# Chunk 2's output product 3 as seven small products, and a new order of copies, differences and GpSimd work around it

## The chip, the cores and the metric

The kernel runs on one core of one Trainium2 chip. The metric is the device time of one execution in microseconds (us). A profile shows one execution: busy times and waits of the engines TensorE (PE, with its weight loads as PEld), VectorE (DVE), ScalarE (ACT), GpSimd (POOL) and of SyncE (SP), which issues most of the transfers.

## What is computed

The reference is an attention without a score matrix, followed by two dense layers with an exact GELU between them:

```python
q_s = softmax(q, axis=-1)            # q, k, v: (8 batches, 8 heads, 576, 64)
k_s = softmax(k, axis=2)             # over the sequence
kv = einsum('bhsd,bhse->bhde', k_s, v)
x = einsum('bhsd,bhde->bhse', q_s, kv)   # then (4608 tokens, 512)
h = x @ w_in                         # w_in: 512 x 2048
g = 0.5 * h * (1 + erf(h / sqrt(2)))
out = g @ w_out                      # w_out: 2048 x 512, float32
```

## The kernel before

The 4608 tokens are cut into nine chunks of 512. Chunk c below 8 holds the first 512 tokens of batch c; chunk 8 holds the last 64 tokens of all eight batches. The program order of every engine is written out by hand: each engine takes its instructions in the order in which the functions below emit them, and waits by semaphores where an operand isn't ready.

For a batch b, `exp_q` and `exp_k` (ScalarE) take the exponentials; `cast_v` turns v into bf16, in four pieces; `kv_mm` multiplies exp(k) and v in two halves of 36 small matmuls (pieces 0 and 1, then 2 and 3), and `kv_norm` (VectorE, L241) or `kv_scale` (ScalarE, L269) divides by k's sums. The sums of exp(q) are made by `reduce_sum` and a reciprocal on VectorE (`q_sums`, or `q_part` twice and `q_rest`). The scaling of exp(q) by them is done on GpSimd (`q_scale`, or `q_scale_parts`, eight instructions of 128x256). `xbar_step` transposes the scaled q with one transfer on SP's queue. `x_all` multiplies kv and the transposed q into four PSUM banks (`x_mm`) and copies these to `xT`, each by ScalarE ("s") or VectorE ("v") as its string says; `x_sums` makes differences of quarters of `xT` on VectorE.

The first dense layer of a chunk is `h_phase`, `h_pairs` or, from chunk 2 on, `h_waves` (L501). There each 2x2 block product is made by seven products instead of eight, `mm(1)` to `mm(7)`, with sums and differences of the quarters of x (`x_sums`) and of the weights (`quad_weights`). `p5_copy`, `e_sum` and `r_sum` combine the products on the way, `gelu` (ScalarE) writes `g`, and `s_parts` (VectorE) makes the differences of `g` that the second layer needs.

The second layer is again seven products, here of 16 matmuls with 256 columns each: in `y_phase` for chunks 1 and 2 (L818), `y_inner` for chunks 3 to 5, `y_inner4` for 6 and 7, `y_last` for 8. The results c11, c12, c21 and c22 are gathered in the tile `yb4` and stored in two halves by `y_store`. `y_inner` makes two of the seven products, 2 and 3, by seven smaller products once more (class `Two`, L734: seven sets of four matmuls with 128 columns). Its weight differences (`two_begin`, `two_begin4`; four GpSimd instructions each) are made once, its activation differences (`sums`, four instructions) once a chunk, for product 3 on GpSimd.

Between chunks stands `next_x` (L1350): x of the next chunk, then kv of the batch after it, while the last products of the present chunk still run. `after(i)` in `y_phase` runs the work that the caller has hung behind product i; L1336 and L1382 are the two callers. GpSimd's work of chunk 2's output is listed at L1384 and L1385: a touch that waits for VectorE's last difference (`touch_s`), `cast_v_all(4)`, `late[3]` (the last weight difference for product 2), `q_scale_parts(4)`. `four_w` holds weight differences for chunks 6 and 7, of which `h_waves` of chunks 3 to 6 make one each, at their start (L562 to L565). In `h_waves` GpSimd is released by the small copy at L622, behind `x_sums(c, (4,))`.

In chunk 0 the last of the second layer (`y_part(15, ...)`, L1291) overlaps with x of chunk 1.

Of the kernel before, what the change touches and what calls it, by code (L numbers as in the profile page):

```python
# [16 lines left out]
def kernel(  # L17
# [11 lines left out]
    nc = tc.nc  # L29
# [173 lines left out]
    def cast_v_all(b):  # L203
        for hp in range(HP):
            cast_v(b, hp, nc.gpsimd)
# [295 lines left out]
    def h_waves(c, mid, first=None):  # L501
# [19 lines left out]
        def mm(m, *qs):  # L521
            for q in qs:
                kind = {5: "B", 3: "B", 2: "C"}.get(m, "A")
                if m in (1, 5):
                    take(kind, q)
                for u in range(2):
                    for k in range(2):
                        if m in plain_w:
                            k0, t0 = plain_w[m]
                            t = 2 * q + t0 + u  # L530
                            w = wi_bf[:, k0 + k, t * 128:(t + 1) * 128]
                        else:
                            t = 2 * (q % 2) + u
                            w = quad["s"][q // 2][:, sum_w[m], k, t * 128:(t + 1) * 128]
                        nc.tensor.matmul(  # L535
                            held[kind, q][:, u], w, mov[m][:, k],
                            start=(m in (1, 5) and u == 0 and k == 0), stop=(k == 1),
                            skip_group_check=True,
                        )
# [19 lines left out]
                nc.scalar.activation(out=g[:, t:t + 2, half], in_=held[kind, q], func=AF.Gelu)  # L559

        vcopy, scopy = nc.vector.tensor_copy, nc.scalar.copy
        if 2 < c < 7:  # L562
            if c == 3:
                four_w.extend(two_begin4())
            four_w[c - 3]()  # L565
        mm(1, 0, 1)
        if first:
# [2 lines left out]
        if mid:  # L570
            seed(1)
            mm(1, 2, 3)
            mm(2, 0, 1)
            gelu("C", 0, 1)
            mm(5, 0, 1)
            p5_copy(0, scopy)
            p5_copy(1, scopy)
            x_sums(c, (3, 4))
            seed(2, vcopy)
            seed(3, vcopy)  # L580
            mm(6, 0, 1)
            e_sum(0)
            e_sum(1)
            mid()
            mm(2, 2, 3)
            gelu("C", 2, 3)
            mm(7, 0, 1)
            r_sum(0)
            r_sum(1)
            mm(3, 0, 1)  # L590
            gelu("B", 0, 1)
            mm(6, 2)
            mm(5, 2, 3)
            p5_copy(2, scopy)
            p5_copy(3, scopy)
            mm(6, 3)
            e_sum(2)
            e_sum(3)
            gelu("r", 0, 1)
            mm(4, 0, 1)  # L600
            gelu("A", 0, 1)
            mm(7, 2, 3)
            r_sum(2)
            r_sum(3)
            s_parts(c, 0, 4, (1,))
            gelu("r", 2, 3)
            mm(3, 2, 3)
            mm(4, 2, 3)
        else:
            mm(5, 0, 1)  # L610
            seed(1)
            p5_copy(0, scopy)
            p5_copy(1, scopy)
            mm(6, 0, 1)
            x_sums(c, (3,))
            if c + 2 <= B:
                q_part(c + 2, 0)
            e_sum(0)
            e_sum(1)
            x_sums(c, (4,))  # L620
            if c + 2 < B:
                nc.gpsimd.tensor_copy(out=scr[:, 2:3], in_=t4[:, 0, 0:1])  # L622
                cast_v_all(c + 2)
            mm(2, 0, 1)
            gelu("C", 0, 1)
            mm(7, 0, 1)
            r_sum(0)
            r_sum(1)
            if c + 2 <= B:
                q_part(c + 2, 1)  # L630
            mm(3, 0, 1)
            for q in (2, 3):
                mm(5, q)
                mm(1, q)
            mm(4, 0, 1)
            gelu("r", 0)
            gelu("B", 0, 1)
            gelu("r", 1)
            seed(2)
            seed(3)  # L640
            gelu("A", 0, 1)
            p5_copy(2, vcopy)
            p5_copy(3, vcopy)
            s_parts(c, 0, 4, (1,))
            mm(6, 2, 3)
            e_sum(2)
            e_sum(3)
            s_parts(c, 0, 4, (2,))
            mm(2, 2, 3)
            gelu("C", 2, 3)  # L650
            mm(7, 2, 3)
            r_sum(2)
            r_sum(3)
            gelu("r", 2, 3)
            mm(3, 2, 3)
            mm(4, 2, 3)
# [151 lines left out]
    def two_begin4():  # L808
        w = w3[:, 4:8].rearrange("p x y n -> p x (y n)")
        s = f32in.tile([128, 4, 512], BF16, tag="zs", name="two", bufs=1)  # L810
        two[4] = Two(4, *(t.rearrange("p x (i n) -> p x i n", i=4) for t in (w, s)))
        return list(two[4].weights())
# [5 lines left out]
    def y_phase(c, ins):  # L818

        act, wgt = y_operands(c)  # L820
        at = {"ya": 2, "yb": 0, "yc": 3} if c == 1 else {"ya": roles["ba"], "yb": roles["bb"], "yc": roles["x0"]}
        pa, pb, pc = (bank(at[n], n) for n in ("ya", "yb", "yc"))
        ysb = [yb4[:, 2 * i:2 * i + 2] for i in range(2)]
        c11, c12 = ysb[0][:, :, 0:HN], ysb[0][:, :, HN:DM]
        c21, c22 = ysb[1][:, :, 0:HN], ysb[1][:, :, HN:DM]

        def halves(ps):
            return ps.rearrange("p (j n) -> p j n", j=2)

        def mm(m, ps, first):  # L830
            for j in range(2):
                for k in range(HK):
                    nc.tensor.matmul(  # L833
                        ps[:, j * HN:(j + 1) * HN], act[m][:, k, j * 128:(j + 1) * 128],
                        wgt[m][:, k, :], start=(first and k == 0 and j == 0),
                        stop=(k == HK - 1), skip_group_check=True,
                    )

        def after(i):
            for fn in ins.get(i, []):  # L840
                fn()

        mm(1, pa, True)
        (nc.vector.tensor_copy if c == 1 else nc.scalar.copy)(out=c11, in_=halves(pa))
        after(1)
        mm(5, pb, True)
        nc.vector.tensor_copy(out=c22, in_=halves(pb))
        after(5)
        mm(6, pa, False)
        tt(halves(pb), halves(pa), c22)  # L850
        after(6)
        mm(2, pc, True)
        tt(c11, c11, halves(pc))
        after(2)
        mm(7, pa, False)
        tt(c22, halves(pa), c22)
        after(7)
        mm(3, pb, False)
        nc.scalar.copy(out=c12, in_=halves(pb))
        y_store(c, 0, ysb[0])  # L860
        after(3)
        mm(4, pa, False)
        nc.scalar.copy(out=c21, in_=halves(pa))
        y_store(c, 1, ysb[1])
        after(4)

    def y_inner(c, nb):

# [403 lines left out]
    def y_part(t, js):  # L1272
        for j in js:
            y_mm(0, yps[j], j, t)
# [13 lines left out]
    cast_v(1, 3, nc.scalar)  # L1288
    kv_norm(1, 0)
    y_part(14, range(J))  # L1290
    y_part(15, (0, 1, 2))  # L1291
    y_out(0, yps[0], 0)
    y_out(0, yps[1], 1, "s")
    x_tile(1, 0, Banks(5), "a")
    x_tile(1, 1, Banks(1), "h")
    x_mm(1, 0)
    kv_mm(1, 1)
    x_evac(1, 0, "s")
    x_evac(1, 1)
    kv_norm(1, 1)  # L1300
    y_part(15, (3,))

# [19 lines left out]
    for m in (3, 2, 4, 1):  # L1322
# [10 lines left out]
    exp_q(2, parts=2)  # L1333
    exp_k(2)

    y_phase(1, {  # L1336
        1: [sums[3], lambda: norm_q(2, 0, 2)],
        6: [lambda: norm_q(2, 1, 2, nc.vector), lambda: cast_v_all(3), lambda: [f() for f in two_begin(3, "vf1")], lambda: xbar_step(2), lambda: exp_q(3)],
        2: [lambda: kv_step(2), lambda: exp_k(3)],
        7: [lambda: q_sums(3)],  # L1340
        3: [lambda: table(AF.Gelu)],
        4: [lambda: load(4), lambda: load_main(5, "q", q), lambda: x_all(2, (3, 4, 1, 5)),
            lambda: kv_step(3, lambda: x_sums(2, (1,))), lambda: x_sums(2, (2,))],
    })

    def touch_s():

        nc.gpsimd.tensor_copy(out=scr[:, 2:3], in_=s12[:, HK - 1, HT:HT + 1])

    def next_x(c, nb, fn=None):  # L1350
        x_all(c + 1, [roles[n] for n in ("x0", "x1", "x2", "x3")], "svss" if fn else "svsv")
        if nb <= B:
            xbar_step(nb)
        if nb < B:
            kv_tiles(nb, (roles["kv0"], roles["kv1"]))
            if fn:
                kv_mm(nb, 0)
                kv_mm(nb, 1)
                x_sums(c + 1, (1,))
                kv_scale(nb)  # L1360
            else:
                kv_step(nb, lambda: x_sums(c + 1, (1,)))
        else:
            x_sums(c + 1, (1,))
        x_sums(c + 1, (2,))
        if fn:
            fn()

    late = []

    def q_late():
# [7 lines left out]
            fn()  # L1379

    h_waves(2, q_late)
    y_phase(2, {  # L1382
        1: [lambda: exp_q(4)],
        5: [lambda: exp_k(4), touch_s, lambda: cast_v_all(4), late[3]],  # L1384
        6: [lambda: q_sums(4), lambda: q_scale_parts(4), lambda: load_late(5), lambda: exp_q(5)],  # L1385
        7: [lambda: table(AF.Gelu)],
        3: [lambda: next_x(2, 4)],
    })
    rest = None
    for c in range(3, B + 1):  # L1390
        h_waves(c, None, rest)
# [37 lines left out]
```

## Time and profile before

| | us |
|---|---|
| median of 3 runs (254.39 to 255.04) | 254.73 |
| the profiled execution | 254.41 |
| its span, first to last instruction | 252.6 |
| mean granted TensorE clock | 0.998 |
| ACT busy | 192.9 |
| one matmul block of 16, 256 columns (product of the output) | 1.75 |
| 16 matmuls of 128 columns (seven small products) | 0.89 |
| four POOL sums for product 3 in chunk 3 | 116.65 to 121.27 |
| chunk 2: first product of the output starts | 85.10 |
| chunk 2: product 3 (yb, second time) | 93.83, 16 matmuls |
| chunk 3: h stage starts | 98.68 |
| chunk 3: first product of the output starts | 111.21 |

Times of places are us from the span's start. In a timeline a row gives start, duration, engine, line, operation, what it writes and reads with shape and type, and in brackets the engine's idle time before it and what ended that. In the chain, a row is a piece of the work that ended last: start, duration, what. Tiles `qa`, `qb`, `qc` are PSUM banks of `h_waves`, `ya`, `yb`, `yba`, `ybb`, `yd`, `ye`, `yf` of the output, `quad_t` the differences of x, `s` and `g` those of g, `two` the operands of the small products.

### The profile page before, as it was taken

The numbers are of one execution on the slowest core, as the hardware profiler recorded it, in microseconds if no ns is written. First come the engines' busy times: TensorE is split into PE (matmuls) and PEld (weight loads), VectorE is DVE, ScalarE is ACT, GpSimd is POOL, SyncE is SP. The second block draws the span as 40 slices with busy tenths as digits, with TensorE's granted clock in tenths as the row PEclk, the third lists the DMA queues.
The fourth block names the chain that finished last, engine by engine and source line by source line (L and its number), as shares of the span: only waits on it lengthen the run. The fifth ranks groups of instructions, "written<-read, shape, count | busy, mean of one in ns | idle before, by whom it ended". The sixth has DMA issues, their size and how long they took to land.

```text
span 252.6 us, 6954 instructions
## 1 busy us (share of the span) xinstructions
PE 245.9 (97%) x2828; PEld 196.5 (78%) x2834; DVE 210.6 (83%) x408; ACT 192.9 (76%) x341; POOL 91.9 (36%) x120
## 2 busy tenths in 40 slices
PE   7899999999999999999999999999999999999994
PEld 3444445447888888889988998899889888998893
DVE  1978698877996987988998889888998989888972
ACT  4785988699887998789888988898882578168811
POOL 1530033000958378405960596049202930330000
PEclk9999999999999999999999999999999999999999
DMA  7999999995189939931992199400700250022015
GB/s 239 394 373 423 404 408 396 402 406 220 27 256 357 347 65 382 285 125 24 401 286 83 21 389 212 176 1 5 249 0 3 84 168 4 0 93 78 0 41 128
DMA packets 43135, 50.25 MB, mean 199 GB/s; under 512 B 20192, under 2 KB 30432, under 8 KB 42848
## 3 DMA queue, kind: packets, MB, share of 16 engines
q1 hardware_dynamic: 42384, 49.13, 57.2%
q10 hardware_dynamic: 720, 0.69, 1.1%
q8 instruction: 22, 0.36, 0.5%
q14 instruction: 9, 0.07, 0.1%
HBM read 36.70 MB, written 9.44 MB: 183 GB/s over the span
## 4 chain that ended last, share of the span: by engine, by line
PE 92%; DMA 4%; DVE 1%; POOL 1%; issue 0%; ACT 0%; SPq 0%; ACTq 0%
PE qa L535 20%; PE ps L412 11%; PE qb L535 10%; PE yba L882 8%; PE ya L833 6%; PE ps L700 5%; PE qc L535 5%; PE yba L954 4%; PE yd L783 4%; PE ye L783 3%; PE yb L833 3%; PE ya L1036 2%; DMA f<-in_v_dram 2%; PE ybb L882 2%; PE yf L783 2%; DMA f<-in_q_dram 2%
## 5 line engine op out<-in xcount | busy, mean ns | idle before, releaser
L535 PEld LDWEIGHTS <-quad_s 128*128 128x128 bf16 x448 | 43.8, 98 | 5.5 <-issue 0.3
L535 PEld LDWEIGHTS <-wi_bf 128*128 128x128 bf16 x336 | 32.8, 98 | 3.9
L535 PE MATMUL qa<-quad_t,quad_s 128*128 128x256 bf16 x224 | 29.4, 272 | 0.0
L412 PE MATMUL ps<-xT,wi_bf 128*128 128x512 bf16 x124 | 27.8, 379 | 0.3
L294 POOL TENSOR_TENSOR e<-e,recq 128x1024 bf16<-128x1024 bf16 (+1 forms) x4 | 9.3, 2333 | 48.5 <-DVE recq L289 48.5
L303 POOL TENSOR_TENSOR e<-e,recq 128x256 bf16<-128x256 bf16 x40 | 25.5, 672 | 0.9 <-ACT ek L189 0.9
L412 PEld LDWEIGHTS <-wi_bf 128*128 128x128 bf16 x128 | 12.4, 98 | 15.2 <-issue 0.6
L455 POOL TENSOR_TENSOR two<-s 128x512 bf16<-128x512 bf16 x10 | 11.6, 1156 | 30.9 <-DVE s L455 30.9
L559 ACT ACTIVATE g<-r 128x512 bf16<-128x512 f32 x28 | 17.3, 632 | 6.7 <-DVE r L455 6.7
L418 ACT ACTIVATE g<-ps 128x512 bf16<-128x512 f32 x32 | 17.6, 602 | 6.1 <-PE ps L412 5.8
L455 DVE TENSOR_TENSOR qb<-qa,r 128x512 f32<-128x512 f32 x28 | 18.1, 693 | 4.6 <-PE qa L535 1.7
L184 ACT ACTIVATE e<-f 128x512 bf16<-128x512 f32 (+1 forms) x42 | 20.4, 557 | 1.8 <-DMA f<-in_q_dram 1.6
L559 ACT ACTIVATE g<-qc 128x512 bf16<-128x512 f32 x28 | 15.2, 594 | 7.2 <-PE qc L535 7.2
L405 ACT CAST xT<-ps 128x512 bf16<-128x512 f32 x25 | 13.3, 595 | 9.2 <-PE ps L378 5.6
L455 DVE TENSOR_TENSOR r<-qa,r 128x512 f32<-128x512 f32 x28 | 18.0, 683 | 0.9 <-PE qa L535 0.7
L201 POOL CAST v_aug<-f 128x576 bf16<-128x576 f32 x25 | 17.2, 726 | 3.3 <-DMA f<-in_v_dram 3.0
L189 ACT ACTIVATE ek<-f 128x2304 bf16<-128x2304 f32 (+1 forms) x10 | 17.3, 1734 | 0.5 <-DMA f<-in_k_dram 0.5
L455 DVE TENSOR_TENSOR yb<-yb,yd 128x128 f32<-128x128 f32 (+2 forms) x35 | 11.9, 358 | 5.4 <-PE yd L783 3.4
L96 ACT ACT_TABLE_LOAD x11 | 14.1, 1283 | 2.9 <-issue 2.7
L288 DVE TENSOR_REDUCE qsum<-e 128x16 f32<-128x1024 bf16 (+1 forms) x8 | 11.8, 1470 | 4.7 <-ACT e L184 4.7
L455 DVE TENSOR_TENSOR s<-g 128x1024 bf16<-128x1024 bf16 (+2 forms) x19 | 11.5, 604 | 4.9 <-ACT g L418 2.8
L535 PE MATMUL qb<-quad_t,quad_s 128*128 128x256 bf16 x112 | 15.5, 272 | 0.0
(152 smaller groups left out, 598.1 us busy)
## 6 DMA issues: line engine op xcount, KB each, us to landing
out_dram<-yb SPq DMA_DIRECT2D x16, 512.0 KB, 3.5
f<-in_k_dram SPq DMA_DIRECT2D x6, 1152.0 KB, 7.5
f<-in_v_dram SPq DMA_DIRECT2D x6, 1152.0 KB, 10.3
f<-in_q_dram SPq DMA_DIRECT2D x6, 1024.0 KB, 11.3
w<-in_moe_w_in_dram SPq DMA_DIRECT2D x6, 512.0 KB, 8.8
f<-in_v_dram SPq DMA_DIRECT2D x8, 288.0 KB, 6.4
f<-in_q_dram SPq DMA_DIRECT2D x4, 512.0 KB, 8.9
w<-in_moe_w_out_dram SPq DMA_DIRECT2D x2, 1024.0 KB, 11.2
```

The costliest lines, as they stand in the source:

```text
L184: nc.scalar.activation(out=dst[:, i], in_=src[:, u], func=AF.Exp)
L189: nc.scalar.activation(out=ek[b % 2][:, i:i + n], in_=st[b]["kf"][:, i:i + n].rearrange("p x (n d) -> p x n d", n=NS), func=AF.Exp,)
L201: eng.tensor_copy(out=o, in_=i)
L303: nc.gpsimd.tensor_tensor(out=e, in0=e, op=ALU.mult, in1=st[b]["recq"][:, j, i:i + 4].unsqueeze(2).to_broadcast([128, 4, D]),)
L412: nc.tensor.matmul(ps, wi_bf[:, dm, t * 128:(t + 1) * 128], st[c]["xT"][:, dm, :], start=(dm == 0), stop=(dm == NDM - 1),)
L418: nc.scalar.activation(out=st[c]["g"][:, t, :], in_=ps, func=AF.Gelu)
L455: eng.tensor_tensor(out=out, in0=in0, in1=in1, op=op)
L535: nc.tensor.matmul(held[kind, q][:, u], w, mov[m][:, k], start=(m in (1, 5) and u == 0 and k == 0), stop=(k == 1), skip_group_check=True,)
L559: nc.scalar.activation(out=g[:, t:t + 2, half], in_=held[kind, q], func=AF.Gelu)
L783: nc.tensor.matmul(getattr(self, at)[:, r * 128:(r + 1) * 128], lhs, rhs, start=first, stop=(i == 3), skip_group_check=True,)
L833: nc.tensor.matmul(ps[:, j * HN:(j + 1) * HN], act[m][:, k, j * 128:(j + 1) * 128], wgt[m][:, k, :], start=(first and k == 0 and j == 0), ...
L882: nc.tensor.matmul(ps[:, j * HN:(j + 1) * HN], act[m][:, k, j * 128:(j + 1) * 128], wgt[m][:, k, :], start=(first and k == 0 and j == 0), ...
```

## The change

In chunk 0, one `y_part(15)` matmul and the copy of its second result go behind the x work of chunk 1. In chunk 1's output, the x copies and both first differences of x for chunk 2 go ahead of c21's copy, and batch 3's reciprocal of the q sums behind them. Chunk 2's output gets a function of its own, `y_first`: product 3 by seven small products, with its sums on GpSimd between the casts of v; batch 4's kv is scaled by ScalarE, and three of the four x copies are ScalarE's. The scaling of batch 4's q and its transpose move to `h_waves` of chunk 3, behind the touch at L622, followed there by the casts, `late[3]` and `four_w[0]`.

```diff
-        if 2 < c < 7:
-            if c == 3:
-                four_w.extend(two_begin4())
+        if c == 3:
+            four_w.extend(two_begin4())
+        elif 3 < c < 7:
             four_w[c - 3]()
...
                 nc.gpsimd.tensor_copy(out=scr[:, 2:3], in_=t4[:, 0, 0:1])
+                if c == 3:
+                    q_scale_parts(4)
+                    xbar_step(4)
                 cast_v_all(c + 2)
+            if c == 3:
+                late[3]()
+                four_w[0]()
...
         mm(4, pa, False)
+        if c == 1:
+            after(4)
         nc.scalar.copy(out=c21, in_=halves(pa))
         y_store(c, 1, ysb[1])
-        after(4)
+
+    def y_first(c, nb):
...
+        mm(1, pa, True)
+        nc.scalar.copy(out=c11, in_=halves(pa))
+        exp_q(nb)
+        mm(5, pb, True)
+        nc.vector.tensor_copy(out=c22, in_=halves(pb))
+        exp_k(nb)
+        touch_s()
+        t3.sums(c, nc.gpsimd, (0, 1))
+        cast_v(nb, 0, nc.gpsimd)
+        t3.sums(c, nc.gpsimd, (2,))
+        cast_v(nb, 1, nc.gpsimd)
+        cast_v(nb, 2, nc.gpsimd)
+        t3.sums(c, nc.gpsimd, (3,))
+        cast_v(nb, 3, nc.gpsimd)
+        load_late(nb + 1)
+        exp_q(nb + 1)
+        mm(6, pa, False)
+        tt(c12, halves(pa), c22)
+        t3.begin(c, bank(roles["bb"], "yf"), bank(roles["kv1"], "yd"))
+        t3.mm(1)
+        t3.add("a", c12)
+        mm(2, pc, True)
+        q_part(nb, 0)
+        tt(c11, c11, halves(pc))
+        mm(7, pa, False, (0,))
+        t3.mm(6)
+        t3.add("b", c12)
+        mm(7, pa, False, (1,))
+        q_part(nb, 1)
+        t3.mm(7)
+        t3.add("c", c12)
+        tt(c22, halves(pa), c22)
+        q_rest(nb)
+        t3.mm(5, 2, 4)
+        table(AF.Gelu)
+
+        def rest():
+            t3.mm(3)
+            t3.add("ed", c12)
+
+        next_x(c, nb, rest, False)
+        y_store(c, 0, ysb[0])
+        mm(4, pa, False)
+        nc.scalar.copy(out=c21, in_=halves(pa))
+        y_store(c, 1, ysb[1])
...
-    y_part(15, (0, 1, 2))
+    y_part(15, (0, 1))
     y_out(0, yps[0], 0)
-    y_out(0, yps[1], 1, "s")
     x_tile(1, 0, Banks(5), "a")
     x_tile(1, 1, Banks(1), "h")
     x_mm(1, 0)
+    y_part(15, (2,))
     kv_mm(1, 1)
     x_evac(1, 0, "s")
     x_evac(1, 1)
+    y_out(0, yps[1], 1, "s")
     kv_norm(1, 1)
...
-        7: [lambda: q_sums(3)],
+        7: [lambda: nc.vector.reduce_sum(out=qsum3, in_=st[3]["eq"], axis=AX.X)],
...
-            lambda: kv_step(3, lambda: x_sums(2, (1,))), lambda: x_sums(2, (2,))],
+            lambda: kv_step(3, lambda: x_sums(2, (1, 2))),
+            lambda: nc.vector.reciprocal(st[3]["recq"], qsum3)],
...
-    def next_x(c, nb, fn=None):
-        x_all(c + 1, [roles[n] for n in ("x0", "x1", "x2", "x3")], "svss" if fn else "svsv")
-        if nb <= B:
+    def next_x(c, nb, fn=None, scaled=True):
+        x_all(c + 1, [roles[n] for n in ("x0", "x1", "x2", "x3")], "svss")
+        if nb <= B and scaled:
             xbar_step(nb)
...
     h_waves(2, q_late)
-    y_phase(2, {
-        1: [lambda: exp_q(4)],
-        5: [lambda: exp_k(4), touch_s, lambda: cast_v_all(4), late[3]],
-        6: [lambda: q_sums(4), lambda: q_scale_parts(4), lambda: load_late(5), lambda: exp_q(5)],
-        7: [lambda: table(AF.Gelu)],
-        3: [lambda: next_x(2, 4)],
-    })
+    y_first(2, 4)
```

More of the change, by code (lines that the diff above doesn't have):

```diff
@@ L862, in y_phase, with halves, mm @@
         mm(4, pa, False)
+        if c == 1:
+            after(4)
         nc.scalar.copy(out=c21, in_=halves(pa))
         y_store(c, 1, ysb[1])
-        after(4)
+    def y_first(c, nb):
+        act, wgt = y_operands(c)
+        pa, pb, pc = (bank(roles[n], "y" + n) for n in ("ba", "bb", "x0"))
+        ysb = [yb4[:, 2 * i:2 * i + 2] for i in range(2)]
+        c11, c12 = ysb[0][:, :, 0:HN], ysb[0][:, :, HN:DM]
+        c21, c22 = ysb[1][:, :, 0:HN], ysb[1][:, :, HN:DM]
+        t3 = two[3]
+        def halves(ps):
+            return ps.rearrange("p (j n) -> p j n", j=2)
+        def mm(m, ps, first, js=(0, 1)):
+            for j in js:
+                for k in range(HK):
+                    nc.tensor.matmul(
+                        ps[:, j * HN:(j + 1) * HN], act[m][:, k, j * 128:(j + 1) * 128],
+                        wgt[m][:, k, :], start=(first and k == 0 and j == 0),
+                        stop=(k == HK - 1), skip_group_check=True,
+                    )
+        mm(1, pa, True)
[41 more added lines that the diff above has]
+        y_store(c, 1, ysb[1])
     def y_inner(c, nb):
@@ L1334 @@
     exp_k(2)
+    qsum3 = small.tile([128, J, H], FP32, tag="qsum", name="qsum")
+    st[3]["recq"] = small.tile([128, J, H], FP32, tag="recq", name="recq")
     y_phase(1, {
@@ L1355, in next_x @@
             kv_tiles(nb, (roles["kv0"], roles["kv1"]))
[L1356 to L1362, printed above, removed]
+            kv_mm(nb, 0)
+            kv_mm(nb, 1)
+            x_sums(c + 1, (1,))
+            kv_scale(nb)
         else:
@@ L1365, in next_x @@
         x_sums(c + 1, (2,))
-        if fn:
-            fn()
+        fn()
     late = []
```

## The prediction, made before the result was known

> **What bounds the kernel now.** I read the page's busy shares and its chain first, then the chain in order of time, then the timeline around the places that the diff touches.
>
> ```profile
> PE 245.9 (97%) x2828; PEld 196.5 (78%) x2834; DVE 210.6 (83%) x408; ACT 192.9 (76%) x341; POOL 91.9 (36%) x120
> ...
> PE 92%; DMA 4%; DVE 1%; POOL 1%; issue 0%; ACT 0%; SPq 0%; ACTq 0%
> ```
>
> TensorE sets the end at a granted clock of 0.998. So an edit is worth what it takes off TensorE's stream or off a gap in it, and costs what it makes TensorE wait. The stream runs at 1.75 us for 16 matmuls of 256 columns (109 ns each) and 0.89 us for 16 of 128 columns (56 ns each). In the chain a block that takes longer than its like holds a wait:
>
> ```profile
> 101.46 0.87 PE qc L535 x8
> 102.34 1.17 PE qa L535 x8
> ...
> 127.15 0.87 PE qc L535 x8
> 128.02 0.88 PE qa L535 x8
> ```
>
> The first pair is chunk 3's h stage, the second the same place of chunk 4. Eight matmuls take 1.17 us instead of 0.87 where they wait for VectorE's e_sum. The whole stage, from its first matmul to the first of the output, is 111.21 - 98.68 = 12.53 us in chunk 3 and 136.59 - 124.37 = 12.22 us in chunk 4: 0.31 us lost. Why e_sum is late stands here:
>
> ```profile
> 98.76 1.15 POOL L455 TENSOR_TENSOR quad_t<-w 128x512 bf16<-128x512 bf16 x1
> 99.05 1.14 DVE L455 TENSOR_TENSOR quad_t<-xT,quad_t 128x512 bf16<-128x512 bf16 x1
> ```
>
> The first is four_w[0]. The difference of x beneath it normally takes 0.42 us; here it ends 0.28 us after GpSimd's operation does. So a VectorE tensor_tensor with both inputs in SBUF waits until the running GpSimd operation is over. The reverse shows too: a q-scaling part takes 0.61 us alone and 0.79 us beside such a VectorE operation. VectorE's sums with a PSUM operand keep their 0.64 us under GpSimd.
>
> **Start of chunk 1 (y_part(15) order, y_out(1) behind the x copy).** Before, the last of seven y_part matmuls starts at 42.25, the x matmuls at 42.56, VectorE's x copy at 43.05 to 43.74, the h matmuls at 43.75. With one y_part matmul (0.216 us) behind the x matmuls, these start at 42.35; VectorE is busy with y_out(0) until 42.93, so its copy ends at 43.56. TensorE, with a matmul more between the small ones, is there by 43.55. Gain 0.18 us, bounds 0 and 0.29 (the whole gap from 43.46). y_out(1) on ScalarE then ends at about 43.95; the bank that it reads is wanted at 44.0. If that cover is gone, it costs some 0.1 us.
>
> **End of chunk 1 (x copies and differences ahead of c21's copy, reciprocal behind them).**
>
> ```profile
> 69.37 2.28 DVE L288 TENSOR_REDUCE qsum<-e 128x32 f32<-128x2048 bf16 x1
> 71.37 0.63 PE L378 MATMUL ps<-qT,kvc 64*64 64x512 bf16 x8
> 72.02 1.22 DVE L403 CAST xT<-ps 128x512 bf16<-128x512 f32 x2
> 72.81 1.96 PE L535 MATMUL qa<-xT,wi_bf 128*128 128x256 bf16 x16
> ```
>
> The two h blocks that come first need x copies 0 and 1, and the second writes the bank of x copy 3, VectorE's second, which ended at 73.24. Without the reciprocal (0.35 us) VectorE can start when the x matmuls let it, some 0.47 us after 71.37 (0.45 and 0.49 us elsewhere), so at 71.84 and done at 73.1. The first h block starts earlier, the second waits for this: gain 0.10 us, bounds 0 and 0.32 (the gap between 72.49, when the kv matmuls are through, and 72.81). c21's copy goes behind two copies on ScalarE, to about 73.46; its bank is wanted at 74.0. SP now has the loads for chunks 4 and 5 (4.3 MB, 12 us at the 357 GB/s of that slice) ahead of the second store of chunk 1: it lands at about 86, and its tile is written again at 89.3. Hidden by 3 us.
>
> **Chunk 2's output (y_first).** Product 3 was 16 matmuls, 1.75 us; now 28 of 128 columns at 56 ns, 1.56 us: -0.19 us. Product 1 of the output started at 85.10; behind five products (8.73 us), six of the seven small sets (1.34) and a change of matmul shape (0.1, as at 121.19) the x matmuls come at 95.27, the kv matmuls at 95.72, and their second half, which needs v cast 3, at 96.09. GpSimd cannot begin before VectorE's last sum for the output:
>
> ```profile
> 89.41 0.19 POOL L1348 CAST scr<-s 128x1 f32<-128x1 bf16 x1 [5.26 <-DVE s L455]
> 89.53 2.49 POOL L201 CAST v_aug<-f 128x576 bf16<-128x576 f32 x4
> ...
> 93.83 1.91 PE L833 MATMUL yb<-wo_bf,s 128*128 128x256 bf16 x16
> 95.67 0.63 PE L378 MATMUL ps<-qT,kvc 64*64 64x512 bf16 x8
> 96.13 0.86 PE L236 MATMUL kv<-v_aug,ek 64*64 64x65 bf16 x72
> 96.92 1.92 PE L833 MATMUL ya<-w,g 128*128 128x256 bf16 x16
> ```
>
> Between 89.53 and cast 3 it now does four sums as well, which in chunk 3 run 116.65 to 121.27 (4.62 us). 4.62 + 4 x 0.61 = 7.06: cast 3 ends at 96.6, TensorE waits 0.5 us. Queued behind that wait are the rest of kv, seven-product set 3 (whose sum is ready at 96.0), product 4 and chunk 3's h stage. Sum: h starts at 99.0 instead of 98.68, +0.32 us; bounds -0.19 (no wait) and +0.5. On SP, chunk 5's v load waits for cast 3 (96.6, before 93.66), with the q load and both stores behind it; v is wanted at 108, so that is hidden. kv scaled by ScalarE is four activations, 0.93 us, under product 4's 1.75 us, as after chunk 3; uncovered it would cost 0.93 us. It takes 0.6 us from VectorE.
>
> **Chunk 3's h stage, its front.** four_w[0] and the q scaling are gone from where VectorE makes x differences, so it should run like chunk 4's: -0.31 us, bounds 0 and -0.36.
>
> **Its tail, where GpSimd's work went.** In us since the stage's first matmul, by chunk 4's rows: GpSimd is released at 4.1; VectorE's differences of g run at 7.65, 9.75, 11.55, 12.15 and, once ScalarE has the last gelu, 13.31; output product 5 wants the last of these by 14.41 (12.22 + 1.75 + 4 x 0.109). GpSimd had only four casts, and was idle for 10.23 us before chunk 3's sums. Now it has eight scaling parts (4.6 us), four casts (2.44), late[3] and four_w[0] (2 x 1.15): free of VectorE it would end at 13.7. But five differences meet it:
>
> ```profile
> 110.54 0.68 DVE L455 TENSOR_TENSOR g<-g 128x1024 bf16<-128x1024 bf16 x1
> 111.14 0.69 DVE L455 TENSOR_TENSOR s<-g,s 128x1024 bf16<-128x1024 bf16 x1
> ...
> 112.29 0.69 DVE L455 TENSOR_TENSOR s<-g 128x1024 bf16<-128x1024 bf16 x1 [0.47 <-ACT g L559]
> ```
>
> They are twice as large as the x difference, which holds GpSimd up by 0.18 us (0.79 - 0.61), and run 0.27 us longer: some 0.45 us each, so late[3] runs to about 14.3 and four_w[0] to about 15.5. The difference ready at 13.31 waits for the one or the other: done at 14.85 (late[3]) or 15.9 (both ahead of it). TensorE waits 0.4 or 1.5 us. In the first case four_w[0] delays the next differences, and with them GpSimd's sums for product 3, which end 0.5 us before set 7 needs them: 0.6 us more there. So 1.0 or 1.5 us; I take 1.2, bounds 0 (GpSimd through by 13.3, or the two don't meet) and 2.3 (each difference behind a full operation). No run here shows a string of such differences against a string of GpSimd operations, so the order in which they take turns is open.
>
> The Trainium skill, "SBUF — State Buffer", section "SBUF: two separate sides", says that VectorE and GpSimd share a port pair by an exclusive lock: whichever starts first keeps it for the whole instruction, also against a VectorE operation with two SBUF inputs. The 0.28 us after GpSimd's end agrees. By a reading of the traces without this lock the tail would cost nothing and the sum below would be -0.27; with it, it costs what was worked out above.
>
> The new transpose of q for chunk 4 leaves SP at about 109, in a time without loads (3.38 us there in chunk 4), and is wanted at 121: hidden by 8 us. In chunk 2 its 7.87 us held the second store back; that is gone, with no gain on TensorE.
>
> **Sum.** -0.18 - 0.10 + 0.32 - 0.31 + 1.2 = +0.93 us on the profiled execution's 254.41 us (252.6 us of span and 1.8 around it). That execution is 0.32 us under the median of 254.73, so I forecast 255.7 us.
>
> **Rivals.**
> - *The tail hides* (GpSimd's last two operations fit between the differences). For it: uncontended it would be through at 13.7, and a difference behind that would be done by 14.25, ahead of 14.41. Against: 1142 ns for the one difference that met a long operation. -0.27: 254.5 us.
> - *GpSimd is nowhere late, the other side*: cast 3 also in time and the tail hidden; then only gains remain, -0.18 - 0.10 - 0.19 - 0.31 = -0.78, with the gaps fully closed -1.1: 253.6 to 254.0 us. It decides from the point where GpSimd's eight operations take under 6.55 us (96.09 - 89.53). Against: 7.06 us by rows that hardly vary (1.16 and 0.67 us).
> - *The lock cascades*: late sums for product 3 push the q scaling and four_w[1] into chunk 4's x differences as well, tail 2.3: +2.0, 256.7 us. Against: GpSimd has a pause of 1.0 us there.
> - *Product 3 saves nothing*, since more weight loads come per column: PEld is 98 ns each, yet 0.89 us for 16 shows no such limit. +0.19 only.
>
> **Chances.** Forecast 0.48 (own range 255.2 to 256.3), tail hidden 0.22, nowhere late 0.19, cascade 0.10, nothing saved 0.01. About 0.3% (0.76 us) is what a measurement of this kernel can tell from no change. Slower by more: 0.36 of the forecast's (its upper three quarters) and the cascade's 0.10, 0.46. Faster by more: 0.17 of *nowhere late* and 0.05 of *the tail hides*, where both start gaps close fully and cast 3 is only half as late, 0.22. Within: 0.32. The range 253.8 to 256.4 us leaves out most of the cascade and the far end of the gains.
>
> **What would show it.** Right: the kv matmuls split by a wait of 0.5 us on GpSimd's v cast; the 1.17 us block at 0.88; differences of g over 1 us beside late[3] and four_w[0], and output product 5 of chunk 3 broken by VectorE. Wrong: chunk 3's differences of g at 0.68 us throughout, or chunk 2's GpSimd row through before 96.1. Then the time falls to one of the rivals.

## The result, and the profile after

| | before | after |
|---|---|---|
| median of 6 runs each, us | 254.34 (254.12 to 255.04) | 256.33 (256.11 to 256.49) |
| profiled execution / its span, us | 254.41 / 252.6 | 256.46 / 254.7 |

The ratio is 1.0075 with a 95% interval of 1.0064 to 1.0085: the changed kernel is 2.0 us slower. The changed page's busy shares and chain:

```profile
PE 246.2 (97%) x2840; PEld 196.3 (77%) x2846; DVE 212.9 (84%) x411; ACT 193.9 (76%) x345; POOL 97.5 (38%) x124
...
PE 83%; DVE 5%; DMA 4%; POOL 3%; issue 2%; ACT 1%; ACTq 0%; POOLq 0%
```

The chain that was 92% TensorE now holds 5% VectorE and 3% GpSimd: in some places the end is set by what these two do. Since TensorE's stream is nearly unbroken, the start of each stage on it shows where (us, worked out from the starts of the first matmuls in the two timelines):

| stage | before | after | difference |
|---|---|---|---|
| start of chunk 2's h stage | 72.81 | 72.91 | +0.10 |
| chunk 2, h stage | 12.29 | 12.39 | +0.10 |
| chunk 2, output | 13.58 | 13.95 | +0.37 |
| chunk 3, h stage | 12.53 | 12.83 | +0.30 |
| chunk 3, output | 13.16 | 14.33 | +1.17 |
| chunk 4, h stage | 12.22 | 12.22 | 0 |
| chunk 4, output | 13.16 | 13.16 | 0 |

They add up to 2.04 us; the span grew from 252.6 to 254.7 us. The largest of them lie in two stretches of the changed kernel's timeline. First, chunk 2's output (a row is start, duration, engine, line, operation, and the idle time before it with what ended that):

```profile
95.47 0.63 PE L378 MATMUL ps<-qT,kvc 64*64 64x512 bf16 x8
...
95.92 0.53 PE L236 MATMUL kv<-v_aug,ek 64*64 64x65 bf16 x38
...
96.14 0.67 POOL L201 CAST v_aug<-f 128x576 bf16<-128x576 f32 x1
...
96.87 0.47 PE L236 MATMUL kv<-v_aug,ek 64*64 64x65 bf16 x34 [0.42 <-POOL v_aug L201]
```

The kv matmuls, one row of 72 before, are cut in two; the second part waits 0.42 us for cast 3 on GpSimd. Next, the end of chunk 3's h stage and the start of its output:

```profile
108.18 1.30 DVE L455 TENSOR_TENSOR qb<-qa,r 128x512 f32<-128x512 f32 x2 [0.58 <-ACT g L559]
...
109.38 1.01 DVE L455 TENSOR_TENSOR s<-s,g 128x1024 bf16<-128x1024 bf16 x1
...
110.32 1.28 DVE L455 TENSOR_TENSOR r<-qa,r 128x512 f32<-128x512 f32 x2
...
111.05 1.20 PE L535 MATMUL qa<-quad_t,wi_bf 128*128 128x256 bf16 x8
...
111.50 1.15 POOL L455 TENSOR_TENSOR two<-wo_bf,two 128x512 bf16<-128x512 bf16 x1
111.52 1.68 DVE L455 TENSOR_TENSOR g<-g 128x1024 bf16<-128x1024 bf16 x1
...
112.61 1.60 POOL L455 TENSOR_TENSOR quad_t<-w 128x512 bf16<-128x512 bf16 x1
...
113.12 1.64 DVE L455 TENSOR_TENSOR s<-g,s 128x1024 bf16<-128x1024 bf16 x1
...
114.68 0.68 DVE L455 TENSOR_TENSOR s<-g 128x1024 bf16<-128x1024 bf16 x1
...
115.42 1.48 PE L956 MATMUL ybb<-wo_bf,s 128*128 128x256 bf16 x12 [0.99 <-DVE s L455]
```

The same place of the kernel before had one unbroken row for product 5:

```profile
112.95 1.91 PE L882 MATMUL ybb<-wo_bf,s 128*128 128x256 bf16 x16
```

In the changed kernel late[3] (111.50) and the difference of g (111.52) start almost together. GpSimd was 0.02 us ahead, and the difference takes 1.68 us instead of 0.68: it ends 0.55 us after late[3] does. Now four_w[0] finds the difference running and takes 1.60 instead of 1.15; the next difference finds four_w[0] and takes 1.64. So they take turns, one operation each. The difference that TensorE needs for product 5 is done at 115.36, and the twelve matmuls behind it start at 115.42. Without a wait they would have followed the first four at 114.27.

### The profile page after: what moved, and what is told of

It reads as the page before. It is cut to its first block, busy times and chain, and to the rows that moved or that the text cites. A ratio compares the mean times of both kernels' runs of the same rounds, so it can differ in the third digit from the quotient of the medians.

```text
span 254.7 us, 6987 instructions
## 1 busy us (share of the span) xinstructions
PE 246.2 (97%) x2840; PEld 196.3 (77%) x2846; DVE 212.9 (84%) x411; ACT 193.9 (76%) x345; POOL 97.5 (38%) x124
## 4 chain that ended last, share of the span: by engine, by line
PE 83%; DVE 5%; DMA 4%; POOL 3%; issue 2%; ACT 1%; ACTq 0%; POOLq 0%
PE qa L535 17%; PE ps L412 11%; PE qb L535 8%; PE yba L956 8%; PE ps L706 6%; PE qc L535 4%; PE yba L1028 4%; PE yd L789 4%; PE ya L839 3%; PE ye L789 3%; DVE s L455 2%; PE ya L1110 2%; DMA f<-in_v_dram 2%; PE kv L236 2%; PE yf L789 2%; PE ybb L956 2%
## 5 line engine op out<-in xcount | busy, mean ns | idle before, releaser
L455 POOL TENSOR_TENSOR two<-s 128x512 bf16<-128x512 bf16 x12 | 13.9, 1157 | 30.9 <-DVE s L455 30.9
L201 POOL CAST v_aug<-f 128x576 bf16<-128x576 f32 x25 | 17.8, 743 | 3.4 <-DMA f<-in_v_dram 3.3
L455 DVE TENSOR_TENSOR yb<-yb,yd 128x128 f32<-128x128 f32 (+2 forms) x38 | 12.9, 356 | 5.7 <-PE yd L789 3.6
L535 PE MATMUL qa<-xT,wi_bf 128*128 128x256 bf16 x112 | 15.5, 273 | 0.0
L559 ACT ACTIVATE g<-qb 128x512 bf16<-128x512 f32 x28 | 15.0, 585 | 0.7 <-PE qb L535 0.7
```

The source lines that it names most:

```text
L201: eng.tensor_copy(out=o, in_=i)
L455: eng.tensor_tensor(out=out, in0=in0, in1=in1, op=op)
L535: nc.tensor.matmul(held[kind, q][:, u], w, mov[m][:, k], start=(m in (1, 5) and u == 0 and k == 0), stop=(k == 1), skip_group_check=True,)
```

## The experiments

Times in the text are medians; "the changed kernel" is the one above, at 1.0075 of the kernel before. Each was timed beside runs of the kernel before, and the ratio is to these.

**1. The scaling of q back in chunk 2's output.**

```diff
-                if c == 3:
-                    q_scale_parts(4)
-                    xbar_step(4)
+                if c == 3:
+                    xbar_step(4)
...
         q_rest(nb)
+        q_scale_parts(nb)
         t3.mm(5, 2, 4)
```

> Changed kernel with one part undone: GpSimd's eight scaling parts of batch 4's q stand behind the casts of v in chunk 2's output again; the transpose stays in chunk 3's h stage. My theory (the loss is GpSimd's work meeting VectorE's differences of g at the end of chunk 3's h stage: 0.6 us in the stage, which takes 12.83 us instead of 12.22, and 1.17 us in its output): the casts, late[3] and four_w[0] are through some 1 us before the second difference of g, the stage falls to 12.2 to 12.5 us and its output to 13.2, the time by 1.4 to 1.8 us to 254.5 to 254.9 us. Rival (the loss is the wait for cast 3 in chunk 2's output, which pushes everything after it, and slower start-up): unchanged at 256.3 us.

Measured: 254.81 us, ratio 1.0011 (1.0002 to 1.0020). Chunk 3's h stage takes 12.48 us and its output 13.16. The two long operations now come before the later differences, in this kernel's timelines of GpSimd and VectorE:

```profile
105.67 1.16 POOL L455 TENSOR_TENSOR two<-wo_bf,two 128x512 bf16<-128x512 bf16 x1
106.78 1.61 POOL L455 TENSOR_TENSOR quad_t<-w 128x512 bf16<-128x512 bf16 x1
```

```profile
110.83 0.68 DVE L455 TENSOR_TENSOR g<-g 128x1024 bf16<-128x1024 bf16 x1
111.43 0.68 DVE L455 TENSOR_TENSOR s<-g,s 128x1024 bf16<-128x1024 bf16 x1
```

The whole 1.17 us of the output is won back by moving GpSimd work that TensorE does not wait for at this place. Chunk 2's output stays at 13.95, so the wait for cast 3 is not where most of the time went.

**2. The same work in another order.**

```diff
                 if c == 3:
+                    late[3]()
+                    four_w[0]()
                     q_scale_parts(4)
                     xbar_step(4)
                 cast_v_all(c + 2)
-            if c == 3:
-                late[3]()
-                four_w[0]()
```

> Changed kernel with the same GpSimd work in chunk 3's h stage in another order: late[3] and four_w[0] (1.15 us each) ahead of the eight scaling parts (0.6 us each) and the casts. If the price is set by how long the one operation is that a difference of g finds running (theory), each difference waits at most 0.6 us, and the time falls by 0.7 to 1.3 us, to 255.0 to 255.6 us. If it is set by how much GpSimd work lies there in all (rival), it stays within 0.3 us of 256.3.

Measured: 255.82 us, ratio 1.0047 (1.0035 to 1.0060): by the ratios 0.7 us better than the changed kernel and 1.2 us slower than the one before. The h stage takes 12.66 and the output 13.95. The time lies between the two theories, a little outside the range of the first. A short operation (here the casts of v, 0.6 us each alone) costs a difference less, but more of the differences meet one:

```profile
111.02 1.07 DVE L455 TENSOR_TENSOR g<-g 128x1024 bf16<-128x1024 bf16 x1
112.01 1.15 DVE L455 TENSOR_TENSOR s<-g,s 128x1024 bf16<-128x1024 bf16 x1
113.08 1.15 DVE L455 TENSOR_TENSOR s<-g 128x1024 bf16<-128x1024 bf16 x1
114.26 1.03 DVE L455 TENSOR_TENSOR s<-s,g 128x1024 bf16<-128x1024 bf16 x1
```

Four in a row take 0.35 to 0.47 us more than 0.68. So both count, the length of the operation and how many there are.

**3. One sum of product 3 on VectorE.**

```diff
+        t3.sums(c, nc.vector, (0,))
         mm(5, pb, True)
...
-        touch_s()
-        t3.sums(c, nc.gpsimd, (0, 1))
+        nc.gpsimd.tensor_copy(out=scr[:, 2:3], in_=t3.s[:, 0, 0, 0:1])
+        t3.sums(c, nc.gpsimd, (1,))
```

> Changed kernel with the first of product 3's four sums made by VectorE (0.42 us, ahead of c22's copy) instead of GpSimd (1.16 us). Theory: cast 3 is done 0.9 us earlier, the kv matmuls of chunk 2 don't wait (0.45 us now), h of chunk 3 starts 0.4 to 0.5 us earlier, the tail is as before: 255.8 to 256.0 us. Rival (VectorE has no room there, and its later copies hold the output's products back): 256.3 us or more.

Measured: 255.70 us, ratio 1.0046 (1.0033 to 1.0058). Chunk 2's output falls to 13.34 us and the kv matmuls are one row again (95.61, 72 of them, 0.81 us). The h stage is 12.30 and the output 14.77, together 27.07 instead of 27.16: the tail's cost is as before, only more of it lies in the output.

**4. Both, 1 and 3.**

> Changed kernel with both: q scaling behind the casts in chunk 2's output, and the first sum of product 3 on VectorE. Theory: the two losses lie one behind the other on TensorE's stream and add up: 1.4 to 1.8 and 0.4 to 0.5 us less, 254.1 to 254.6 us, the kernel before at 254.3 or a little better. Rival (what GpSimd no longer does in the tail comes back as contention with the x differences at the start of chunk 3's h stage): 255 us or more.

Measured: 254.13 us, ratio 0.9989 (0.9980 to 0.9998). Chunk 2's output takes 13.34, chunk 3's stages 12.39 and 13.16 us. The two losses add up, as forecast, and without them the stage that holds the small products of product 3 gains 13.58 - 13.34 = 0.24 us (0.19 was forecast for them). This version is 0.1% faster than the kernel before.

**5. The edits around chunk 1 alone, on the kernel before.** The diff is the part of the change that touches `y_part(15)`, `after(4)` and the reciprocal.

> Kernel before with the edits at the start and end of chunk 1 alone (order of y_part(15), y_out(1) behind the x copy, x copies and differences ahead of c21's copy, reciprocal behind them). By the prediction's two terms: -0.18 and -0.10 us, 254.1 to 254.2 us. Rival (the transposed q of chunk 2 lands later behind the earlier loads and the second h block still waits for VectorE's last x copy, so that the gain is lost before chunk 2's output): no change within 0.1 us, with chunk 2's output starting 41.35 us after the first h matmul of chunk 1 as in both kernels so far.

Measured: 254.27 us, ratio 0.9994 (0.9985 to 1.0003). This doesn't tell a gain of 0.28 us from none. In its profile chunk 1's output and the x work behind it take 14.53 us instead of 14.81, and chunk 2's h stage 12.39 instead of 12.29; chunk 2's output starts 41.18 us after the first h matmul of chunk 1. Over the kernels with these edits, apart from those of experiments 7 and 8, that distance lies between 41.18 and 41.45 us (41.35 before), and chunk 2's h stage takes 12.39 or 12.40 us in all of them but that of experiment 9, which has the order at chunk 1's end as before (12.25).

**6. four_w[0] made in chunk 1, on the kernel before.**

```diff
-        if 2 < c < 7:
-            if c == 3:
-                four_w.extend(two_begin4())
+        if 3 < c < 7:
             four_w[c - 3]()
...
-lambda: [f() for f in two_begin(3, "vf1")],
+lambda: [f() for f in two_begin(3, "vf1")], lambda: four_w.extend(two_begin4()), lambda: four_w[0](),
```

> Kernel before with one thing moved: four_w[0], the 1.15 us GpSimd operation at the start of chunk 3's h stage, made in chunk 1's output. Theory (that operation alone makes the x difference, and with it e_sum, late): chunk 3's h stage 12.2 to 12.3 us instead of 12.53, the time by 0.2 to 0.3 us to 254.15 to 254.3. Rival (VectorE's kv_norm there, 0.9 us, is what makes e_sum late): 12.4 to 12.5 us, no change.

Measured: 254.09 us, ratio 0.9983 (0.9975 to 0.9992). Chunk 3's h stage takes 12.37 us: half of the 0.31 us was that one operation. The other half is most likely VectorE's scaling of kv, which this kernel still has. For that speaks experiment 1: there ScalarE scales kv, the q scaling again runs beside the x differences, and e_sum starts 2.45 us into the stage, as in chunk 4; here it starts at 2.74. No run changes the scaling of kv alone. By the stages the moved line is worth 0.2 us (12.37 for 12.53, and 12.24 for 12.29 in chunk 2); the ratio's interval goes from 0.2 to 0.6 us.

**7. As 4, with four_w[0] made in chunk 1.**

> The kernel with q scaling behind the casts and the first sum on VectorE, and four_w[0] made in chunk 1's output as well, so that chunk 3's h stage has only the casts and late[3] on GpSimd. There the first difference of g took 1.25 us beside four_w[0] and the stage 12.39 us. Theory: the difference takes 0.68 us, the stage 12.2 to 12.3, the time falls by 0.1 to 0.2 us to 253.9 to 254.1. Rival (that delay was hidden, or four_w[0] costs as much in chunk 1): no change.

Measured: 254.22 us, ratio 0.9992 (0.9983 to 1.0000). Chunk 3's h stage is 12.23 us, as expected, but chunk 2's is 12.92 instead of 12.40. There the changed order puts both first differences of x for chunk 2 beside it, and the second takes 1.19 us; in the kernel of 6 the second comes later and takes 0.57 us (stage 12.24 us). What was won in chunk 3 is lost in chunk 2.

**8. Only the short operations in chunk 3's h stage.** late[3] goes behind cast 3 in chunk 2's output, four_w[0] to chunk 1's output.

```diff
         cast_v(nb, 3, nc.gpsimd)
+        late[3]()
...
-            if c == 3:
-                late[3]()
-                four_w[0]()
```

> Changed kernel with both 1.15 us operations taken out of chunk 3's h stage (late[3] behind cast 3 in chunk 2's output, four_w[0] in chunk 1's), the eight scaling parts and the casts left there. Theory (each difference of g waits for the operation that runs, and the long ones do most of it): the stage loses up to 0.4 us to the short ones, chunk 3's output 0.1 us at most, 254.6 to 255.1 us. Rival (the scaling parts are what costs): 255.7 us or more.

Measured: 255.63 us, ratio 1.0047 (1.0034 to 1.0059), by the time nearer the rival. By stages it splits: chunk 3's h stage 12.83 us, as in the changed kernel, its output 13.16, but chunk 2's h stage 12.94, the 0.55 us of experiment 7 that this kernel has for its own. So the long operations cost the 1.17 us of the output, and the 0.6 us within the h stage is there without them: the second difference meets a cast and r_sum stands behind it, at the same places of the stage as in the changed kernel.

```profile
110.06 1.01 DVE L455 TENSOR_TENSOR s<-s,g 128x1024 bf16<-128x1024 bf16 x1
111.00 1.27 DVE L455 TENSOR_TENSOR r<-qa,r 128x512 f32<-128x512 f32 x2
```

**9. The best parts together**: 4 and 6, with the order at chunk 1's end as before.

> Product 3 of chunk 2 by small products, its first sum on VectorE, q scaling behind the casts, four_w[0] made in chunk 1's output, and the order at chunk 1's end as in the kernel before (differences of x apart, copies behind c21's). The stage times of the runs so far, put together: chunk 1's output 14.81, chunk 2's h stage 12.24, its output 13.34, chunk 3's h stage 12.23, its output 13.16 us, against 14.81, 12.29, 13.58, 12.53, 13.16 before: 0.6 us less than the kernel before, a ratio of 0.9970 to 0.9985. Rival (the four_w[0] operation costs chunk 2's h stage 0.53 us as it did beside the changed order of x differences): no better than 0.999.

Measured: 254.35 us, ratio 0.9994 (0.9986 to 1.0003). The stages came out as expected (12.25, 13.34, 12.23, 13.16), so the rival's 0.53 us is not there, and its profiled execution has the shortest span of all the profiles, 252.2 us, 0.4 less than before. But the 0.6 us does not show in the medians, where the time is what the rival said, and why stays open. The start of a single execution varies by more than that (first h matmul of chunk 1 between 43.61 and 44.54 us over the profiles).

**10. The price by itself, in chunk 4.**

```diff
                 cast_v_all(c + 2)
+            if c == 4:
+                for i in range(6):
+                    four_w[0]()
```

> Kernel before with six GpSimd operations more (four_w[0] made again, 1.15 us each, same values) behind the casts of v in chunk 4's h stage, where nothing else is changed and GpSimd idles until chunk 4's output: the disputed price by itself. Theory (a difference of g and a GpSimd operation take turns, each blocked for the whole of the other's): the five differences that meet them end 0.55 us after the operation that they find, the last two with one operation between; the h stage takes 12.6 to 13.1 us instead of 12.22, chunk 4's output up to 14.3 to 14.6 instead of 13.16, the time 1.2 to 2.2 us more, 255.7 to 256.7. Rival (the loss in chunk 3 came from its later start and from ScalarE's part, not from GpSimd): 0.2 us at most.

Measured: 256.19 us, ratio 1.0063 (1.0050 to 1.0076). Chunk 4's h stage takes 12.88 us and its output 14.31; chunks 2 and 3 are as in the kernel before (13.58, 12.52, 13.16). From this kernel's timelines of VectorE and GpSimd:

```profile
134.38 1.44 DVE L455 TENSOR_TENSOR s<-s,g 128x1024 bf16<-128x1024 bf16 x1
135.74 1.28 DVE L455 TENSOR_TENSOR r<-qa,r 128x512 f32<-128x512 f32 x2
136.93 1.67 DVE L455 TENSOR_TENSOR g<-g 128x1024 bf16<-128x1024 bf16 x1
138.53 1.64 DVE L455 TENSOR_TENSOR s<-g,s 128x1024 bf16<-128x1024 bf16 x1
140.09 0.68 DVE L455 TENSOR_TENSOR s<-g 128x1024 bf16<-128x1024 bf16 x1
```

```profile
131.32 8.30 POOL L455 TENSOR_TENSOR quad_t<-w 128x512 bf16<-128x512 bf16 x6
```

Six operations of 1.15 us, together 6.9 us at most, take 8.30, and the three differences shown that meet them 1.44 to 1.67. The sums with a PSUM operand between them (135.74, two in 1.28 us) are untouched. Nothing else was changed here, and the stages lose 0.66 and 1.15 us, where chunk 3 of the changed kernel lost 0.61 and 1.17 against chunk 4's.

## Why the prediction was right, and where it was off

The forecast was slower, by 0.93 us, from GpSimd's work meeting VectorE's differences at the end of chunk 3's h stage. The sign, the place and the mechanism held: experiments 1 and 10 show them from both sides. The size was half of what came, 2.0 us. Of the 1.1 us that it fell short, 0.58 is the tail, 0.48 the two terms around chunk 1 and 0.05 chunk 2's output. The 256.33 us lies 0.07 us inside the range, and that is in part luck: the forecast was added to a median of 254.73 us, and the kernel before came out at 254.34 here. By size alone the rival *the lock cascades* (+2.0 us) fits, but not by its mechanism: it has late GpSimd work run on into chunk 4's x differences, and chunk 4's two stages are unchanged. By its steps:

- *Chunk 2's output*, +0.32: measured +0.37. The wait for cast 3 is there (0.42 us, 0.5 forecast), and the stage saves 0.24 us where it is gone (0.19 forecast for the small products).
- *Front of chunk 3's h stage*, -0.31: the e_sum wait is gone. The first difference of g starts 7.66 us into the stage, 7.94 before, 7.65 in chunk 4. The forecast put it down to four_w[0] and the q scaling; experiment 6 shows that four_w[0] is only half of it, and by experiment 1 the q scaling need not cost anything there. The rest most likely came with kv's scaling by ScalarE, which the forecast had not counted here.
- *The tail*, +1.2: this is the term that was mis-sized, 12.83 - 12.22 + 1.17 = 1.78 us. The 1.17 us in the output lies between the two cases worked out, and the order of turns is that of the second: strictly one after the other. What the step left out is the loss inside the h stage, 0.61 us. It was reckoned from the last difference alone, with the stage at 12.22; but r_sum stands on VectorE's queue behind the second difference, and TensorE's last products wait for r_sum (in experiment 10 the profile names this wait, 0.33 us). The second difference met a cast and took 1.01 us instead of 0.68, which is about 0.35 of the 0.61 us. The other 0.26 is there in experiment 1 as well (12.48), where VectorE's e_sum of the second half starts 8.91 us into the stage instead of 8.56 (8.93 in the changed kernel, the row at 108.18), on a ScalarE semaphore. That wait appears when all four sums of product 3 are GpSimd's (experiments 1 and 8, the changed kernel) and not with one on VectorE (3 and 7). Why the program then waits for a later ScalarE instruction was not found.
- *The start and end of chunk 1*, -0.18 and -0.10: nothing of it arrived in the changed kernel, which was 0.20 us late at chunk 2's output. Before the first edit it already ran 0.17 us late (first transposes of q at 40.09 instead of 39.92), which is no part of the change. From there to the first h matmul of chunk 1 it took 3.86 us (3.83 before). Between the first h matmul of chunk 1 and chunk 2's output it took 41.35 us, as before. What the x work behind chunk 1's output gained (14.70 us instead of 14.81) chunk 2's h stage lost again. The x matmuls waited for the transposed q as before, and chunk 2's second h block started just behind the end of VectorE's last x copy; experiment 5 leaves open whether anything remains.
- *Stores, loads and the later transpose* at nothing: no wait on them turned up at the places named.

The Trainium skill, "SBUF — State Buffer", section "SBUF: two separate sides", on which one sentence of the prediction leaned, says that the shared port pair goes to whichever operation starts first, for its whole length. The runs agree: 1.68 and 1.64 us instead of 0.68, ending 0.55 us after the GpSimd operation.

## What to carry to other kernels

When an idle engine is given more work, ask what runs on its neighbour at that time, not only whether the time is free: here GpSimd's 10.2 us without work before chunk 3's sums were never filled up (4.7 us were left), and the work put there still cost 1.8 us, since VectorE's differences of g and GpSimd's operations did not run side by side. Cost such a meeting for every operation queued behind it on the slowed engine, not only for the one whose result is due last. And move one thing at a time: by the stages, one GpSimd operation put in another place (experiment 6) took off 0.2 us, where the whole bundle added 2.0.

## What the runs showed of the hardware that was not expected

Where VectorE's differences from SBUF and GpSimd's operations both queue up, they alternate one to one in the changed kernel, in experiment 3 and at the end of experiment 10's six operations: neither keeps the other out for two operations running. In the two meetings that began almost level, GpSimd was ahead by 0.02 us (111.50 against 111.52) and by 0.03 us (experiment 10, 136.90 against 136.93), and both times the difference took 1.68 or 1.67 us. A GpSimd operation of 1.15 us that finds a difference running takes 1.48 to 1.60 us.
